# Two loads for x of tile 0, and the first k weights and router weights on ScalarE's queue

## The chip, the core and the metric

The kernel runs on one core of a Trainium2 chip. The metric is the device time of the whole kernel in microseconds (us). TensorE (PE) multiplies, VectorE (DVE), ScalarE (ACT) and GpSimd (POOL) do the elementwise work, and SyncE (SP) mostly issues DMAs; ScalarE can issue DMAs too, on a queue of its own. Both queues feed the same 16 DMA engines of the core.

## The reference

The input x has 2048 rows of 640 values in bf16. It is normalized, goes through linear attention with 32 heads of 20 values, and the rows that a small router picks get an expert's output added. What is computed, in short:

```python
xn = layernorm(x)
q, k, v = split(xn @ wqkv)               # 32 heads of 20
pq, pk = phi(q), phi(k)                  # phi(t) = where(t > 0, t + 1, exp(t)) + 1e-6
num = pq @ (pk^T v);  den = pq . sum(pk)  # for each head
A = (num / (den + 1e-6)) @ wo
r = x @ w_r                              # router: the 8 rows with the largest r
y = (silu(x_sel @ w_gate) * (x_sel @ w_up)) @ w_down * sigmoid(r_sel)
B = x, with y added to those 8 rows
out = x + A + B
```

## The kernel before

The rows are cut into 16 tiles of 128 (one row for each partition). The instructions of all engines are written out by hand in one function, and each engine executes its own in the order in which they are written; an instruction that waits holds up all that follow it on its engine.

The start, which is where the change lies, does this. The function `ld` (L103) issues every load: on SP's queue the tiles 0, 1 and 2 of x, the first half of the k weights (`wkh[0]`, 320 of 640 columns of tile `wk`), tile 3 of x, the second half of the k weights, then the tiles 4 to 15 by three loads of four tiles. On ScalarE's queue goes the load of the router weights `wr`, five rows of 128 values, 1.2 KB, after the load of the activation tables (L106). The weights are laid on the partitions, five rows of 320 values each; one half is 400 KB. One tile of x is 160 KB.

TensorE begins with matmuls on constants that nobody reads (`warm4`, L121): 512 and 256 columns in f32. Then it transposes `wr` into a column (L133), and a second block of 512 columns of `warm4` follows. ScalarE copies that column into the k weights' tile (L135), behind the second half, so that the products of the second half give the router's value r beside the keys (321 columns instead of 320).

For each tile the layer norm takes VectorE's statistics of the two halves of a row (`ln_a` L151, `ln_b` L154), their sum (`ln_g` L157), ScalarE's Ln and Exp for the inverse deviation (`ln_r` L160 and L161) and VectorE's normalization (`ln_xn` L165). Tiles 0 to 3 are then transposed on TensorE (`tr_mm`, L174) and copied to `xnT` by ScalarE or VectorE (`tr_cp`, L181 and L183); later tiles go through a transposing DMA (L186). `K` (L208) multiplies the transposed tile by the two halves of the k weights, ScalarE takes Exp (L224) and Relu (L227), VectorE joins them to `pk` (L243), and `G` (L248, L253) sums the products of the normalized x and `pk` over all tiles in PSUM.

The order around the start, on TensorE, is: warm-up blocks, `wr`, warm-up block, both transposes of tile 0 and the first of tile 1, `K(0)` with the first half of the weights, and so on:

```python
    warm4(512)
    warm4(256)
    pe.transpose(PS[:, 3, :].bitcast(BF16)[:, 0:KC], wr[:], ident[0:KC, 0:KC])
    warm4(512)
    act.copy(wkh[1][:, :, HW], PS[:, 3, :].bitcast(BF16)[:, 0:KC])
```

After the 16 tiles the kernel computes q, the routing and the expert, the merged output weights and the output, tile by tile, with TensorE busy nearly all the time. None of that is written differently.

Of the kernel before, what the change touches and what calls it, by code (L numbers as in the profile page):

```python
# [7 lines left out]
P = 128  # L8
S = 2048
D = 640  # L10
# [28 lines left out]
def kernel(  # L39
# [13 lines left out]
    pe, dve, act, pool, sp = nc.tensor, nc.vector, nc.scalar, nc.gpsimd, nc.sync  # L53

    x_v = A_x[0].rearrange("(t p) d -> p t d", p=P)
    out_v = out[0].rearrange("(t p) d -> p t d", p=P)
    wqkv_v = A_wqkv.rearrange("(kc p) n -> p kc n", p=P)
# [9 lines left out]
    def st(shape, dt, name, tag=None):  # L67
        return sb.tile(shape, dt, name=name, tag=tag or name)

    XX = st([P, T, 2, D], BF16, "XX")  # L70
# [27 lines left out]
    HW = 320  # L98
    wkh = [wk[:, :, 0:HW], wk[:, :, HW + 64 :]]


    def ld(eng, dst, src):
        eng.dma_start(dst, src)  # L103

    ld(sp, XX[:, 0, 1, :], x_v[:, 0, :])
    act.preload_act_table_set("natural_log_exp_and_others")  # L106
    dve.memset(zero[:], 0.0)
    dve.memset(MVf[:], 0.0)
    wr = st([KC, P], BF16, "wr")
    ld(act, wr[:], B_w_r.rearrange("(kc p) -> kc p", p=P))  # L110
    ld(sp, XX[:, 1, 1, :], x_v[:, 1, :])
    ld(sp, XX[:, 2, 1, :], x_v[:, 2, :])
    ld(sp, wkh[0], wqkv_v[:, :, D : D + HW])
    ld(sp, XX[:, 3, 1, :], x_v[:, 3, :])
    ld(sp, wkh[1][:, :, 0:HW], wqkv_v[:, :, D + HW : 2 * D])
    for a, b in ((4, 8), (8, 12), (12, 16)):
        ld(sp, XX[:, a:b, 1, :], x_v[:, a:b, :])
    sp.dma_start_transpose(xnT[:, 0:4, S - P : S], zero[:])

# [820 lines left out]
```

## Time and profile before

| what | value |
|---|---|
| time, median of 3 runs | 106.92 us (106.86 to 107.23) |
| the profiled execution | 107.24 us, of which the span of the trace is 105.5 us |
| TensorE busy | 100.8 us (96%) |
| VectorE, ScalarE, GpSimd busy | 82.5, 69.1, 17.1 us |
| chain that ended last | TensorE 89%, DMA 5% |
| SP's queue, ScalarE's queue | 19.42 MB in 22536 packets, 0.05 MB in 186 packets |

Times in the profile are microseconds from the start of the span; a mean or a duration of one instruction is in ns where it stands without a point. PE is the matmul side of TensorE and PEld its weight loads; a matmul's record is longer than its distance to the next one, since they are pipelined. SPq and ACTq are the DMA issues of SP and ScalarE: their length is that of the issuing instruction, not that of the transfer. In square brackets stands for how long the engine sat idle before the instruction, and what released it. A row with "x3" merges three instructions that follow each other.

### The profile page before, as it was taken

The page shows a single profiled execution, that of the slowest core. Times are in us where ns is not written, and L with a number is a line of the kernel's source. Part 1 is how long each engine was busy: PE and PEld are TensorE (multiplying, and loading weights), DVE is VectorE, ACT ScalarE, POOL GpSimd, SP SyncE. Part 2 cuts the span into 40 slices and gives each one's busy share as a digit, 9 for nine tenths or more (in the row PEclk, how much of TensorE's full clock was granted, in tenths as well). Part 3 has the DMA queues.
Part 4 walks back from the last instruction along what each step waited for, and adds up shares of the span by engine and source line. Part 5 has one row for each costly group of instructions (what it writes and reads, how often), then busy time and mean ns, then how long its engine had stood idle before and what let it go on. Part 6 is the DMA issues. An engine that isn't in the chain of part 4 may idle for free.

```text
span 105.5 us, 2548 instructions
## 1 busy us (share of the span) xinstructions
PE 100.8 (96%) x916; PEld 63.7 (60%) x924; DVE 82.5 (78%) x187; ACT 69.1 (65%) x171; POOL 17.1 (16%) x60
## 2 busy tenths in 40 slices
PE   6989999999999999999999999999999999999980
PEld 3356666666666666667556555655567767777760
DVE  1886999988888898873798995727988997888870
ACT  4359965666666666888597999978993997000000
POOL 7800000430000000000000583300002400000500
PEclk9999999999999999999999999999999999999999
DMA  2899947333555775889998999911630125896343
GB/s 83 228 336 378 319 74 57 77 65 79 117 134 122 115 132 123 185 245 365 237 402 253 362 349 383 321 46 50 229 132 9 29 90 182 193 356 220 124 128 124
DMA packets 23023, 19.65 MB, mean 186 GB/s; under 512 B 10594, under 2 KB 21474, under 8 KB 23010
## 3 DMA queue, kind: packets, MB, share of 16 engines
q1 hardware_dynamic: 22536, 19.42, 64.5%
q8 instruction: 7, 0.11, 0.5%
q0 software_dynamic: 288, 0.01, 0.3%
q10 hardware_dynamic: 186, 0.05, 0.2%
q14 instruction: 6, 0.05, 0.2%
HBM read 13.80 MB, written 3.65 MB: 165 GB/s over the span
## 4 chain that ended last, share of the span: by engine, by line
PE 89%; DMA 5%; issue 1%; SPq 1%; DVE 1%; DVEq 0%
PE PS L208 21%; PE PS L474 21%; PE PS L739 19%; PE PS L248 15%; DMA wk<-in_A_wqkv_dram 5%; PE PS L253 4%; PE PS L695 2%; PE PS L655 1%; SPq L103 1%; PE PS L538 1%; PE PS L717 1%; PE PS L267 1%; PE PS L666 1%; PE PS L174 1%; DVE o L752 1%
## 5 line engine op out<-in xcount | busy, mean ns | idle before, releaser
L208 PE MATMUL PS<-wk,xnT 128*128 128x320 bf16 (+1 forms) x160 | 25.2, 300 | 0.5 <-DMA wk<-in_A_wqkv_dram 0.5
L248 PE MATMUL PS<-pk,XX 128*128 128x512 bf16 x75 | 22.7, 379 | 0.0
L474 PE MATMUL PS<-xnT,wq 128*128 128x512 bf16 x97 | 22.4, 380 | 0.2
L739 PE MATMUL PS<-Mb,pqT 128*128 128x320 bf16 (+4 forms) x165 | 22.1, 295 | 0.0
L224 ACT ACTIVATE ek<-PS 128x320 bf16<-128x320 f32 x32 | 14.1, 441 | 9.9 <-PE PS L208 9.9
L739 PEld LDWEIGHTS <-pqT 128*128 128x128 bf16 x165 | 15.9, 98 | 6.4 <-issue 0.3
L208 PEld LDWEIGHTS <-xnT 128*128 128x128 bf16 x160 | 15.3, 98 | 7.1 <-issue 0.5
L474 PEld LDWEIGHTS <-wq 128*128 128x128 bf16 x100 | 11.4, 118 | 9.1 <-issue 0.2
L243 DVE SCALAR_TENSOR_TENSOR pk<-ek,rk 128x640 bf16<-128x640 bf16 x16 | 13.1, 819 | 4.8 <-ACT rk L227 4.5
L529 DVE SCALAR_TENSOR_TENSOR pqT<-qe,qr 128x512 bf16<-128x512 bf16 x20 | 13.5, 683 | 2.1 <-ACT qr L481 2.0
L480 ACT ACTIVATE qe<-PS 128x512 bf16<-128x512 f32 x20 | 12.2, 609 | 3.3 <-PE PS L474 3.3
L253 PE MATMUL PS<-pk,XX 128*128 128x128 bf16 x64 | 14.0, 219 | 0.3
L227 ACT ACTIVATE rk<-PS 128x320 bf16<-128x320 f32 x32 | 14.0, 437 | 0.0
L248 PEld LDWEIGHTS <-XX 128*128 128x128 bf16 x80 | 7.8, 98 | 8.1
L481 ACT ACTIVATE qr<-PS 128x512 bf16<-128x512 f32 x20 | 12.2, 608 | 0.0
L748 DVE TENSOR_TENSOR o<-PS,XX 128x640 bf16<-128x640 f32 x11 | 9.0, 822 | 2.9 <-PE PS L739 2.0
L198 ACT ACTIVATE XX<-XX,MR,SR 128x640 bf16<-128x640 bf16 x11 | 9.4, 913 | 0.0
L151 DVE BATCH_NORM_STATS2 stats<-XX 128x6 f32<-128x320 bf16 x16 | 7.4, 464 | 2.2 <-DMA XX<-in_A_x_dram 2.2
L165 DVE TENSOR_SCALAR XX<-XX,MVf,SR 128x640 bf16<-128x640 bf16 (+2 forms) x17 | 7.2, 432 | 0.9 <-ACT SR L161 0.9
L259 POOL MEMSET XX<- 128x1 bf16 x18 | 1.9, 108 | 36.0 <-DVE XX L165 14.0
L154 DVE BATCH_NORM_STATS2 stats<-XX 128x6 f32<-128x320 bf16 x16 | 7.7, 479 | 0.0
L253 PEld LDWEIGHTS <-XX 128*128 128x128 bf16 x64 | 6.3, 98 | 0.8
(113 smaller groups left out, 96.0 us busy)
## 6 DMA issues: line engine op xcount, KB each, us to landing
out_dram<-o SPq DMA_DIRECT2D x15, 160.0 KB, 2.0
XX<-in_A_x_dram SPq DMA_DIRECT2D x3, 640.0 KB, 7.8
wg<-in_B_w_gate_dram SPq DMA_DIRECT2D x5, 384.0 KB, 9.1
wu<-in_B_w_up_dram SPq DMA_DIRECT2D x5, 384.0 KB, 6.1
wd<-in_B_w_down_dram SPq DMA_DIRECT2D x1, 1920.0 KB, 10.8
wk<-in_A_wqkv_dram SPq DMA_DIRECT2D x2, 400.0 KB, 5.1
wv<-in_A_wqkv_dram SPq DMA_DIRECT2D x5, 160.0 KB, 3.2
wq<-in_A_wqkv_dram SPq DMA_DIRECT2D x1, 800.0 KB, 5.2
```

The source lines that it names most:

```text
L198: act.activation(XX[:, t, 1, :], XX[:, t, 1, :], AF.Identity, bias=MR[:, t : t + 1], scale=SR1[:, t : t + 1])
L208: pe.matmul(PS[:, b + h, off(t, h) : off(t, h) + w], lhsT=xnT[:, kc, t * P : (t + 1) * P], rhs=wkh[h][:, kc, 0:w], start=(kc == 0), stop=( ...
L224: act.activation(phis[t][0][:, h * HW : (h + 1) * HW], phi_src(t, h, b), AF.Exp)
L227: act.activation(phis[t][1][:, h * HW : (h + 1) * HW], phi_src(t, h, b), AF.Relu)
L243: dve.scalar_tensor_tensor(out=pk[:, t, :], in0=ek[:], scalar=1.0, in1=rk[:], op0=ALU.min, op1=ALU.add)
L248: pe.matmul(PS[:, a, :], lhsT=lhsT, rhs=pk[:, t, 0:512], start=(t == 0), stop=(t == T - 1),)
L253: pe.matmul(PS[:, 5, a * P : (a + 1) * P], lhsT=lhsT, rhs=pk[:, t, 512:D], start=(t == 0 and a == 0), stop=(t == T - 1), skip_group_check= ...
L474: pe.matmul(PS[:, bank, :], lhsT=by5(wq[:, kc, :])[:, m, :], rhs=xnT[:, kc, tb * TBLK : (tb + 1) * TBLK], start=(kc == 0), stop=(kc == KC ...
L480: act.activation(e, PS[:, bank, :], AF.Exp)
L481: act.activation(r, PS[:, bank, :], AF.Relu)
L529: dve.scalar_tensor_tensor(out=pqT[:, m, tb * TBLK : (tb + 1) * TBLK], in0=e, scalar=1.0, in1=r, op0=ALU.min, op1=ALU.add,)
L739: pe.matmul(PS[:, b, o : o + c1 - c0], lhsT=pqT[:, kc, t * P : (t + 1) * P], rhs=Mb[:, kc, c0:c1], start=(kc == 0), stop=(kc == KC - 1))
```

## The change

Tile 0 of x is loaded by two DMAs of 64 partitions, one on SP's queue and one on ScalarE's, there ahead of the load of the activation tables. The first half of the k weights moves from SP's queue to ScalarE's, ahead of the router weights. SP's queue keeps the tiles 1, 2 and 3 of x, now without the k weights between them, and the second half of the k weights. The tiles 8 to 15 come by one load instead of two.

```diff
-    ld(sp, XX[:, 0, 1, :], x_v[:, 0, :])
+    ld(sp, XX[0:64, 0, 1, :], x_v[0:64, 0, :])
+    ld(act, XX[64:P, 0, 1, :], x_v[64:P, 0, :])
     act.preload_act_table_set("natural_log_exp_and_others")
     dve.memset(zero[:], 0.0)
     dve.memset(MVf[:], 0.0)
     wr = st([KC, P], BF16, "wr")
+    ld(act, wkh[0], wqkv_v[:, :, D : D + HW])
     ld(act, wr[:], B_w_r.rearrange("(kc p) -> kc p", p=P))
     ld(sp, XX[:, 1, 1, :], x_v[:, 1, :])
     ld(sp, XX[:, 2, 1, :], x_v[:, 2, :])
-    ld(sp, wkh[0], wqkv_v[:, :, D : D + HW])
     ld(sp, XX[:, 3, 1, :], x_v[:, 3, :])
     ld(sp, wkh[1][:, :, 0:HW], wqkv_v[:, :, D + HW : 2 * D])
-    for a, b in ((4, 8), (8, 12), (12, 16)):
+    for a, b in ((4, 8), (8, 16)):
         ld(sp, XX[:, a:b, 1, :], x_v[:, a:b, :])
     sp.dma_start_transpose(xnT[:, 0:4, S - P : S], zero[:])
```

The diff adds a line to the file, so all lines behind L105 have a number that is one higher after the change.

ScalarE's first instructions in the program before (XX is x, wk the k weights, wr the router weights; in brackets what the instruction waits for):

```order
L106 ACT_TABLE_LOAD
L103 DMA wr<-in_B_w_r_dram 5x128
L135 COPY wk<-PS 128x5 [waits PE_49]
L160 ACTIVATE lnv<-MVf,eps_88 128x1 [waits DVE_49]
L161 ACTIVATE SR<-lnv 128x1 [waits Activation_49]
```

And after the change:

```order
L103 DMA XX<-in_A_x_dram 64x640
L107 ACT_TABLE_LOAD
L103 DMA wk<-in_A_wqkv_dram 128x5x320
L103 DMA wr<-in_B_w_r_dram 5x128
L136 COPY wk<-PS 128x5 [waits PE_49]
L161 ACTIVATE lnv<-MVf,eps_88 128x1 [waits DVE_49]
L162 ACTIVATE SR<-lnv 128x1 [waits Activation_49]
```

The issue of wr has moved from first to third on ScalarE's queue; the copy that needs the transposed wr, and the layer norm behind it, stand in the same order.

SP's first instructions before (DMAHW0_49 and the like are the semaphores of earlier DMAs, of which there are eight in turn):

```order
L103 DMA XX<-in_A_x_dram 128x640 x3
L103 DMA wk<-in_A_wqkv_dram 128x5x320
L103 DMA XX<-in_A_x_dram 128x640
L103 DMA wk<-in_A_wqkv_dram 128x5x320
L103 DMA XX<-in_A_x_dram 128x4x640
L103 DMA XX<-in_A_x_dram 128x4x640 [waits DMAHW0_49]
L103 DMA XX<-in_A_x_dram 128x4x640 [waits DMAHW1_49]
```

And after:

```order
L103 DMA XX<-in_A_x_dram 64x640
L103 DMA XX<-in_A_x_dram 128x640 x3
L103 DMA wk<-in_A_wqkv_dram 128x5x320
L103 DMA XX<-in_A_x_dram 128x4x640 [waits DMAHW0_49]
L103 DMA XX<-in_A_x_dram 128x8x640 [waits DMAHW1_49]
```

One load of k weights has gone from between the loads of x, and the load of tiles 4 to 7, the ninth DMA of the program instead of the eighth, now waits until the first half of tile 0 has landed.

TensorE's, VectorE's and GpSimd's instructions stand in the same order before and after. On TensorE the transpose of wr waits for wr's DMA, as before:

```order
L121 MATMUL PS<-const-float32-0.0 128x512
L121 MATMUL PS<-const-float32-0.0 128x256
L133 LDWEIGHTS wr [waits DMAHW3_49]
L133 MATMUL PS<-ident,wr 128x5 [waits Pool_49]
L121 MATMUL PS<-const-float32-0.0 128x512
L174 LDWEIGHTS XX [waits DVE_49]
```

This is the program before; in the program after, the same rows have line numbers higher by one, and the third waits for DMAHW7_49, the semaphore that wr's DMA has there.

## The prediction

> **What bounds the kernel now.** I read the page first, then the chain that ended last in order of time, then the timelines of the first 8 us engine by engine, then the DMA issues.
>
> The page's head, and the first steps of the chain (start, length, what):
>
> ```profile
> span 105.5 us, 2548 instructions
> PE 100.8 (96%) x916; PEld 63.7 (60%) x924; DVE 82.5 (78%) x187; ACT 69.1 (65%) x171; POOL 17.1 (16%) x60
> ...
> 0.81 0.40 SPq L103
> 1.21 0.06 issue
> 1.27 0.42 SPq L103
> 1.73 0.42 SPq L103
> 2.20 4.88 DMA wk<-in_A_wqkv_dram
> 7.12 0.43 PE PS L208 x2
> ```
>
> TensorE is the bound. Before 7.12 us the chain is not TensorE's: it is SP issuing three x loads one after the other and then the load of the first half of the k weights, which takes 4.88 us to land. Afterwards TensorE hardly rests. In the table by stretches (busy time of each engine) it is busy 12.77 of the 12.88 us that follow:
>
> ```profile
> 7.12:20.00 12.88, 12.77 (x98) 8.30 (x100) 11.32 (x29) 10.26 (x36) 0.76 (x8) 1.00 0.79 196
> 20.00:52.00 32.00, 31.79 (x232) 20.41 (x235) 24.94 (x62) 22.14 (x67) 2.88 (x17) 1.00 0.67 155
> ```
>
> So whatever moves the first product of K(0), now at 7.12, moves the end by nearly the same amount, and nothing later has the slack to give it back. The question is only when that product starts. TensorE's and its weight loader's timelines up to it:
>
> ```profile
> 3.67 0.18 PE L133 MATMUL PS<-ident,wr 5*128 5x5 bf16 x1
> 3.79 2.08 PE L121 MATMUL PS<-const-float32-0.0 128*128 128x512 f32 x2
> 5.65 0.95 PE L174 MATMUL PS<-ident,XX 128*128 128x128 bf16 x7
> 7.12 0.43 PE L208 MATMUL PS<-wk,xnT 128*128 128x320 bf16 x2 [0.52 <-DMA wk<-in_A_wqkv_dram]
> ...
> 5.41 0.93 PEld L174 LDWEIGHTS <-XX 128*128 128x128 bf16 x7 [1.12 <-DVE XX L165]
> 6.54 0.10 PEld L208 LDWEIGHTS <-xnT 128*128 128x128 bf16 x1 [0.20 <-ACT xnT L181]
> ```
>
> TensorE works in written order: the small transpose of the router weights wr (L133), the second warm-up block (L121), the transposes of x (L174), then K. The transposed x is there at 6.54; the k weights keep TensorE idle for 0.52 us, and that is all that an earlier wk can win. ScalarE's part:
>
> ```profile
> 0.80 1.28 ACT L106 ACT_TABLE_LOAD   x1 [0.80 <-PEq L924]
> 0.83 0.58 ACTq L103 DMA_DIRECT2D wr<-in_B_w_r_dram  x1
> 3.89 0.18 ACT L135 COPY wk<-PS 128x5 bf16<-128x5 bf16 x1 [1.81 <-PE PS L133]
> ```
>
> wr is issued at 0.83 and never keeps TensorE waiting: L133 at 3.67 follows the first warm-up block. The copy L135 waits for L133, and the layer norm's Ln and Exp of tile 0 stand behind it on ScalarE.
>
> **The change part by part.** First what the loads cost now, from the timeline of SP's issues and from the DMA issues of short windows (count, KB each, us from issue to landing; issued at 1.27, 2.20, 2.68 and 3.24):
>
> ```profile
> 2.20 0.43 SPq L103 DMA_DIRECT2D wk<-in_A_wqkv_dram  x1
> 2.68 0.52 SPq L103 DMA_DIRECT2D XX<-in_A_x_dram  x1
> 3.24 0.43 SPq L103 DMA_DIRECT2D wk<-in_A_wqkv_dram  x1
> ...
> XX<-in_A_x_dram SPq DMA_DIRECT2D x1, 160.0 KB, 2.3
> wk<-in_A_wqkv_dram SPq DMA_DIRECT2D x1, 400.0 KB, 4.9
> XX<-in_A_x_dram SPq DMA_DIRECT2D x1, 160.0 KB, 4.8
> wk<-in_A_wqkv_dram SPq DMA_DIRECT2D x1, 400.0 KB, 5.4
> ...
> 2.20:5.01 2.81, 2.81 (x6) 0.94 (x4) 1.96 (x7) 0.68 (x3) 2.52 (x9) 1.00 0.91 234
> 5.00:7.12 2.12, 1.61 (x9) 0.89 (x8) 2.06 (x7) 1.50 (x5) 0.30 (x2) 1.00 1.09 335
> ```
>
> The second row of the middle part and the third differ in one thing: the 160 KB of tile 1 stand behind a load of their own size and land 2.3 us after their issue; the 160 KB of tile 3 stand behind wk on the same queue and take 4.8 us, landing at 7.48, 0.4 us after wk (2.20 + 4.9 = 7.1). A small load behind a large one on one queue lands with or after the large one. The change puts wr in exactly that place: its 1.2 KB go out on ScalarE's queue behind half of x's tile 0 and behind wk's 400 KB.
>
> *x of tile 0 in two halves.* Two loads of 64 partitions instead of one of 128. VectorE's first statistics wait for it:
>
> ```profile
> 3.02 0.49 DVE L151 BATCH_NORM_STATS2 stats<-XX 128x6 f32<-128x320 bf16 x1 [1.76 <-DMA XX<-in_A_x_dram]
> ```
>
> A gain here is hidden: the second warm-up block holds TensorE up to 5.65, and L174's weights were there at 5.41. If the halves land later, up to 0.2 us is hidden now, and more if wr is late. I cost it at nothing.
>
> *wk on ScalarE's queue.* Issues there take 0.58 us by the wr row, 0.43 by the wk row; so the half of x goes out at 0.83, wk at about 1.3 to 1.5 instead of 2.20, and wr at 1.8 to 2.1 instead of 0.83. The table load doesn't hold them up: wr's issue ran beside it. Then wk shares the DMA engines with tiles 0 to 3 of x on SP's queue. Bounds for its landing: 2.3 us after the issue like a lone x load (3.7), or 5.4 like the second half of wk (6.9). In between, by volume: 640 KB of x and 400 KB of wk are 1.06 MB; packets of SP's queue flow from about 1.8 (the row below is the window from 1.7 to 2.1 us: packets, MB, share of 16 engines), and at 234 to 335 GB/s this takes 3.2 to 4.5 us, so 5.0 to 6.3. I take 5.8, nearest to the upper rows, since the second half of wk joins before the end.
>
> ```profile
> q1 hardware_dynamic: 36, 0.05, 56.3%
> ```
>
> *wr behind it.* It lands when wk does, at L = 5.8 instead of in time for 3.67. Now everything on TensorE is in order behind L133: L133 at L + 0.05, the warm-up block 0.12 later, L174 at L133 + 1.98 (5.65 − 3.67), K at L174 + 0.95 (from 5.65 to 6.60, where the seven transposes end and xnT is there). Together K starts at L + 2.98 = 8.78, with wk long landed. Against 7.12 that is **+1.66 us**. ScalarE's copy, Ln, Exp and VectorE's normalization, queued behind L133 too, need L135's 0.18, then 5.41 − 3.89 = 1.52 us from copy to L174's weights, and are ready before the warm-up block is through: they add nothing.
>
> *The clock.* The warm-up block exists to keep TensorE busy. The same transposes of 128x128 have two durations, up to 6.3 us (first group) and from 7.4 (second), each row giving count, duration in ns and the starts of the first and last:
>
> ```profile
> L174 PE MATMUL PS<-ident,XX x7: 314/314/314, 5.7 to 6.3; 128*128 128x128 bf16 x7
> L174 PE MATMUL PS<-ident,XX x3: 218/219/219, 7.4 to 7.5; 128*128 128x128 bf16 x3
> L121 PE MATMUL PS<-const-float32-0.0 x6: 634/1061/1222, 0.8 to 4.8; 128*128 128x512 f32 x4, 128*128 128x256 f32 x2
> ```
>
> The granted-clock column reads 1.00 in both stretches, so these durations are the evidence: the full rate came between 6.3 and 7.4, 2.5 to 3.6 us after the second warm-up block's start at 3.79. After the change TensorE idles from 3.7 to 5.85 and the block starts at 5.97; the full rate then comes at 8.5 to 9.6, and K, from 8.78, runs up to 0.8 us at about half rate, which costs 0 to 0.4 us. I take **+0.2**, the middle.
>
> *The rest.* SP loses one issue ahead of tiles 1 to 3, so these and the second half of wk go out about 0.5 us earlier; with K at 8.78 this buys nothing (the second half of wk landed at 3.24 + 5.4 = 8.64 even before). The load of tiles 4 to 7 now waits for the first half of x, which lands about when SP gets there. Tiles 8 to 15 come as one load of 1280 KB; the ninth L151 is tile 8's:
>
> ```profile
> L151 DVE BATCH_NORM_STATS2 stats<-XX x9: 440/486/496, 3.0 to 19.1; 128x6 f32<-128x320 bf16 x9
> ...
> 3.72 2.86 SPq L103 DMA_DIRECT2D XX<-in_A_x_dram  x3
> XX<-in_A_x_dram SPq DMA_DIRECT2D x1, 640.0 KB, 8.9
> ```
>
> It ran at 19.1. The last of the three 640 KB loads, issued before 6.6, landed 8.9 us later, by 15.5 at the latest; the same bytes in two loads land about then, and over 3 us of cover hide them. Nothing.
>
> **The sum.** 1.66 + 0.2 = +1.9 us. The profiled execution took 107.24 us (span 105.5 and 1.7 around it), so it would give 109.1; it lies 0.3 above the median of 106.92, and I put the forecast on the median: **108.8 us**. With L between 5.0 and 6.9 it is 107.8 to 109.9.
>
> **The rivals.**
>
> *wr slips past wk (faster).* Should its few packets not be held by the 400 KB, L133 stays at 3.67 and only the 0.52 us in front of K goes: 106.92 − 0.5 = 106.4. It decides at L = 4.14: below that K starts no later than 7.12. For it: wr has five rows only, and no trace shows a small load behind a large one on ScalarE's queue. Against: the 4.8 us of tile 3 on SP's queue.
>
> *Nothing arrives sooner or later (same).* The bytes before K are the same, and the transfer share was 0.91 and 1.09 of 16 engines from 2.2 to 7.1 us: a second queue adds no engine. wk then lands near 7.1 still, and wr, if its packets get in between the others, before 3.7: 106.9. The Trainium skill says as much (DMA: Bandwidth & Descriptors, Rules for kernel authors): two transfers of disjoint partition halves serialize on the same engines and are not worth it, and spreading loads over issuing engines saves only issue time. The 0.91 agrees; the issue rows (three of about 0.45 us ahead of wk) show why the saved issue time may still count here.
>
> *The clock falls back (slower still).* If the idle 2.2 us wipe out what TensorE had earned, the count starts anew at 5.97. Before, the full rate came 5.5 to 6.6 us after the first warm-up matmul at 0.8 (the last row of that fence); so it would come at about 12, and K's products from 8.78 would run 3.2 us at half rate, losing 1.6: 106.92 + 1.66 + 1.6 = 110.2. For it: TensorE was busy almost all the time from 0.8 and still needed until after 6.3. Against: the gap is less than half of that. The Trainium skill (TensorE: Matmul & The Clock Gate, Part 1) has a free-running window of about 3.4 us that must be busy before the clock is released; by that the release would come at the end of the first busy window after 5.97, an estimate of 9.4 to 12.8, costing 0.3 to 2.0 us; the trace shows no window's edges.
>
> **How the numbers follow.** About 0.5% is what a measurement of this kernel can tell from no change, so faster is below 106.4, slower above 107.45. The forecast has 0.76, of which 0.04 (L just above 4.1) counts as same; wr slipping past 0.10 (0.08 faster, 0.02 same); nothing moves 0.07 (same); the clock falls back 0.07 (slower). Faster 0.08, same 0.02 + 0.07 + 0.04 = 0.13, slower 0.72 + 0.07 = 0.79. The range from 106.9 to 110.0 leaves out the gain and the worst of the clock, together under 0.2.
>
> **What would show it.** In the profile after: the transpose of wr at 5 to 7 us instead of 3.67, its weight load put down to the DMA of wr; the x transposes 2 us behind it; the copy of wr on ScalarE waiting until then; K's first product at 8 to 10 us with no wait on wk, which landed around 6; and all later stretches as they were. It is wrong if the transpose of wr stays near 3.7, or if TensorE after K(0) makes up more than a few tenths.

## The result and the profile after

| what | before | after |
|---|---|---|
| time, median | 106.89 us (106.57 to 107.23) | 111.52 us (109.73 to 112.55), 4 runs |
| ratio to before | | 1.034 (95% interval 1.027 to 1.040) |
| the profiled execution | 107.24 us, span 105.5 | 112.55 us, span 110.8 |
| first product of K | 7.12 us | 11.39 us |

Slower, by 4.6 us in the medians and by 3.6 us by the ratio, where 1.9 was forecast; the median is outside the range. The times after scatter far more than those before, and the ratio leaves out the highest of them as slow runs, so both are given. The profile after is that of the highest of the four times.

TensorE's timeline in that profile, start, length and what it waited for:

```profile
8.52 0.18 PE L134 MATMUL PS<-ident,wr 5*128 5x5 bf16 x1 [4.78 <-DMA wr<-in_B_w_r_dram]
8.63 2.08 PE L122 MATMUL PS<-const-float32-0.0 128*128 128x512 f32 x2
10.50 0.95 PE L175 MATMUL PS<-ident,XX 128*128 128x128 bf16 x7
11.39 0.71 PE L209 MATMUL PS<-wk,xnT 128*128 128x320 bf16 x2
11.89 0.53 PE L175 MATMUL PS<-ident,XX 128*128 128x128 bf16 x3
12.21 2.63 PE L209 MATMUL PS<-wk,xnT 128*128 128x320 bf16 x12
```

TensorE idles 4.78 us for wr, whose transpose now runs at 8.52 instead of 3.67. Behind it come the warm-up block and the transposes of x at the old distance, and K follows without the old wait for wk. The last row is the second loss: the same twelve products of K take 2.63 us, where the profile before has

```profile
7.56 1.86 PE L208 MATMUL PS<-wk,xnT 128*128 128x320 bf16 x12
```

ScalarE's issues, its copy of wr and VectorE's first work after:

```profile
0.81 0.60 ACTq L103 DMA_DIRECT2D XX<-in_A_x_dram  x1
1.48 0.82 ACTq L103 DMA_DIRECT2D wk<-in_A_wqkv_dram  x1
2.34 0.68 ACTq L103 DMA_DIRECT2D wr<-in_B_w_r_dram  x1
8.74 0.18 ACT L136 COPY wk<-PS 128x5 bf16<-128x5 bf16 x1 [6.00 <-PE PS L134]
3.56 0.49 DVE L152 BATCH_NORM_STATS2 stats<-XX 128x6 f32<-128x320 bf16 x1 [2.30 <-DMA XX<-in_A_x_dram]
9.37 0.99 DVE L166 TENSOR_SCALAR XX<-XX,MVf,SR 128x256 bf16<-128x256 bf16 x3 [3.82 <-ACT SR L162]
```

The chain that ended last shows the change in two rows; wr's load takes the place that wk's had:

```profile
2.34 6.14 DMA wr<-in_B_w_r_dram
8.70 2.01 PE PS L122 x2
```

In the table by stretches (busy times of PE, PEld, DVE, ACT and POOL, then granted clock, DMA share, GB/s) the clock falls:

```profile
3.70:7.08 3.38, 0.04 (x1) 0.00 (x0) 1.81 (x6) 0.00 (x0) 1.30 (x4) 1.00 0.96 285
7.08:13.90 6.82, 5.38 (x22) 2.98 (x23) 3.24 (x10) 3.43 (x13) 0.20 (x2) 0.50 1.15 329
13.90:20.00 6.10, 6.10 (x52) 4.27 (x51) 4.90 (x14) 5.20 (x19) 0.20 (x2) 1.00 0.01 3
```

After 3.4 us in which TensorE did next to nothing it is granted half its clock, for 6.8 us, and K's first products at 11.39 fall into that time.

### The profile page after: what moved, and what is told of

It is laid out like the page before. It is cut to its first block, busy times and chain, and to the rows that moved or that the text cites. A ratio compares the mean times of both kernels' runs of the same rounds, so it can differ in the third digit from the quotient of the medians.

```text
span 110.8 us, 2558 instructions
## 1 busy us (share of the span) xinstructions
PE 102.3 (92%) x924; PEld 64.5 (58%) x924; DVE 82.5 (74%) x187; ACT 69.1 (62%) x171; POOL 17.3 (16%) x60
## 4 chain that ended last, share of the span: by engine, by line
PE 88%; DMA 6%; issue 1%; ACT 1%; DVE 1%; ACTq 1%; DVEq 0%
PE PS L209 21%; PE PS L475 20%; PE PS L740 18%; PE PS L249 16%; DMA wr<-in_B_w_r_dram 6%; PE PS L254 3%; PE PS L122 2%; PE PS L696 2%; PE PS L175 1%; PE PS L656 1%; PE PS L539 1%; PE PS L718 1%; PE PS L268 1%; ACT L107 1%; PE PS L667 1%
## 5 line engine op out<-in xcount | busy, mean ns | idle before, releaser
L209 PE MATMUL PS<-wk,xnT 128*128 128x320 bf16 (+1 forms) x160 | 26.2, 308 | 0.0
L249 PE MATMUL PS<-pk,XX 128*128 128x512 bf16 x80 | 23.5, 379 | 0.0
```

What stands on the lines that cost most here:

```text
L209: pe.matmul(PS[:, b + h, off(t, h) : off(t, h) + w], lhsT=xnT[:, kc, t * P : (t + 1) * P], rhs=wkh[h][:, kc, 0:w], start=(kc == 0), stop=( ...
L249: pe.matmul(PS[:, a, :], lhsT=lhsT, rhs=pk[:, t, 0:512], start=(t == 0), stop=(t == T - 1),)
```

## The experiments

**wr first.** The two loads on ScalarE's queue exchanged:

```diff
-    ld(act, wkh[0], wqkv_v[:, :, D : D + HW])
     ld(act, wr[:], B_w_r.rearrange("(kc p) -> kc p", p=P))
+    ld(act, wkh[0], wqkv_v[:, :, D : D + HW])
```

> The changed kernel with the two loads on ScalarE's queue exchanged: wr goes out ahead of the k weights, everything else as changed. Theory 1 (the whole loss is that wr stands behind the k weights and TensorE, in order, waits for it): the transpose of wr is back at 3.7 us, TensorE waits only for the k weights, whose landing was 7.1 before and 8.3 after, so K starts at 6.6 to 8.3 and the time is 106.4 to 108.2, most likely 107. Theory 2 (the k weights or x arrive too late on two queues): the loss stays for the most part, 109 to 111.5.

Measured: 110.16 us median, 107.74 to 112.02; ratio 1.029 (1.022 to 1.037). A miss for theory 1 in its strong form. Its profiled run, of 107.74 us:

```profile
3.68 0.18 PE L134 MATMUL PS<-ident,wr 5*128 5x5 bf16 x1
6.29 0.99 PE L175 MATMUL PS<-ident,XX 128*128 128x128 bf16 x7 [0.72 <-DVE XX L166]
7.64 0.43 PE L209 MATMUL PS<-wk,xnT 128*128 128x320 bf16 x2 [0.37 <-DMA wk<-in_A_wqkv_dram]
wk<-in_A_wqkv_dram ACTq DMA_DIRECT2D x1, 400.0 KB, 5.3
```

wr no longer holds TensorE, but the transposes of x are 0.64 us late and wk lands at 7.6: it is now the third issue on ScalarE's queue, at 2.30. So wr's place isn't the only loss. This profile is of the lowest of the four times; the others, 109.61, 110.70 and 112.02, have no trace (their mean granted clocks were 0.984, 0.984 and 0.969), and what they lost is not shown.

**wr behind wk, alone.** The kernel before, with wr's load on SP's queue right behind the first half of wk:

```diff
-    ld(act, wr[:], B_w_r.rearrange("(kc p) -> kc p", p=P))
     ld(sp, wkh[0], wqkv_v[:, :, D : D + HW])
+    ld(sp, wr[:], B_w_r.rearrange("(kc p) -> kc p", p=P))
```

> The kernel before, with one thing moved: the load of wr goes on SP's queue right behind the first half of the k weights, nothing on ScalarE's. Theory 1: this alone brings most of the loss; wr lands at or after 7.1 us with the k weights, the transpose of wr follows, K starts 3 us behind it at 10 or later: 109.5 to 111.5. Theory 2 (the split of x or the sharing of two queues): wr's place costs little, 107 to 107.5.

Measured: 109.83 us, 109.41 to 110.29; ratio 1.025 (1.020 to 1.030). With nothing split and nothing on a second queue, wr's place alone costs most of the loss. wr was expected at 7.1 or later with wk; it was there at 6.1, and wk landed at 6.2 here (4.0 us from its issue):

```profile
6.12 0.18 PE L133 MATMUL PS<-ident,wr 5*128 5x5 bf16 x1 [2.38 <-DMA wr<-in_B_w_r_dram]
8.98 0.72 PE L208 MATMUL PS<-wk,xnT 128*128 128x320 bf16 x2
9.81 2.71 PE L208 MATMUL PS<-wk,xnT 128*128 128x320 bf16 x12
```

Against the profiled run before, K starts 1.86 us later and the time, 110.29, is 3.05 us longer: the other 1.19 us come behind K's start, with all twelve products at the slow rate.

**wr's transpose later on TensorE.** All loads as changed; the transpose stands ahead of `K(1, (0,), 4, KA)`, the copy ahead of `ln_r(2)`, both through another bank of PSUM:

```diff
-    pe.transpose(PS[:, 3, :].bitcast(BF16)[:, 0:KC], wr[:], ident[0:KC, 0:KC])
-    act.copy(wkh[1][:, :, HW], PS[:, 3, :].bitcast(BF16)[:, 0:KC])
...
+    pe.transpose(PS[:, 5, :].bitcast(BF16)[:, 0:KC], wr[:], ident[0:KC, 0:KC])
     K(1, (0,), 4, KA)
+    act.copy(wkh[1][:, :, HW], PS[:, 5, :].bitcast(BF16)[:, 0:KC])
     ln_r(2)
```

> The changed kernel with all its loads; only the transpose of wr and the copy of its result are written later: on TensorE ahead of K(1) with the first half of the weights, on ScalarE behind the four copies of the transposed tiles. Theory 1: wr still lands at 5.5 to 8.5 us, but the warm-up block, tile 0's layer norm and its transposes no longer stand behind it; K(0) starts when the k weights land, 6.7 to 8.3, and the time is 106.6 to 108.5. If instead the late arrival of the k weights and not the order on TensorE is the loss, K(0) starts no earlier than 10 and the time stays at 110 or more.

Measured: 108.37 us, 107.45 to 109.11; ratio 1.015 (1.007 to 1.023). The loads go out as in the changed kernel, and over half of the loss goes, since tile 0's transposes and K no longer stand behind wr. wk landed at 6.5 in this profile, which is of the lowest time; when wr landed isn't seen, as at 8.03 nothing waits for it:

```profile
6.26 0.99 PE L173 MATMUL PS<-ident,XX 128*128 128x128 bf16 x7 [0.81 <-DVE XX L164]
7.09 0.44 PE L207 MATMUL PS<-wk,xnT 128*128 128x320 bf16 x2
8.03 0.17 PE L358 MATMUL PS<-ident,wr 5*128 5x5 bf16 x1
```

So it is the order on TensorE that turns a late wr into a late K. Two of the four times, 109.07 and 109.11, still lie 2 us above before; they have no trace.

**The gap filled.** The changed kernel with five more warm-up blocks ahead of wr's transpose:

```diff
     warm4(256)
+    for _ in range(5):
+        warm4(256)
     pe.transpose(PS[:, 3, :].bitcast(BF16)[:, 0:KC], wr[:], ident[0:KC, 0:KC])
```

> The changed kernel with five more warm-up blocks of 256 columns between the first warm-up blocks and the transpose of wr: TensorE is busy for 2.4 us (full clock) to 4.8 us (half clock) of the time in which it waited for wr. Theory 1 with the clock falling back as its second part: wr lands as late as in the changed kernel and K starts 2 to 3 us after it, but the granted clock stays full or the transposes and K's first products run at the distance of the full clock, so 0.7 to 1.9 us of the loss go: 109.3 to 110.8 against 111.5. If the clock plays no part, the time stays within 0.5 us of the changed kernel.

Measured: 110.16 us, 109.92 to 110.97; ratio 1.031 (1.025 to 1.037), 1.4 us under the changed kernel's median. The transposes of x and the products run at the full rate, and K starts 2.01 us behind wr's transpose instead of 2.87:

```profile
7.38 0.17 PE L136 MATMUL PS<-ident,wr 5*128 5x5 bf16 x1
9.39 0.43 PE L211 MATMUL PS<-wk,xnT 128*128 128x320 bf16 x2
9.83 1.86 PE L211 MATMUL PS<-wk,xnT 128*128 128x320 bf16 x12
PE PS L211 <- DMA xnT<-XX: 0.5, 1, 0.5
```

The last row, from its waits, is new: TensorE waits 0.5 us for the transposing DMA of a later tile, which it never did in the four profiles of the changed kernel. Why it comes here is not shown.

**The split, alone.** The kernel before with x's tile 0 in two halves:

```diff
-    ld(sp, XX[:, 0, 1, :], x_v[:, 0, :])
+    ld(sp, XX[0:64, 0, 1, :], x_v[0:64, 0, :])
+    ld(act, XX[64:P, 0, 1, :], x_v[64:P, 0, :])
```

> The kernel before with the split of x's tile 0 alone: 64 partitions on SP's queue, 64 on ScalarE's ahead of the table load, then wr; the k weights and the rest stay on SP's queue. What the runs have shown so far: with the split the halves landed at 3.45 us instead of 2.99, and in the run with wr first VectorE got the transposes' input to TensorE 0.6 us later. Theory A (the split delays the layer norm by its two issues and the shared engines): tile 0 lands at 3.3 to 3.5, the first transpose is at 6.0 to 6.3 instead of 5.65, TensorE idles between warm-up and transposes, K at 7.1 to 7.6: 106.9 to 107.6 where the clock stays full, 1.7 more where it falls to half for 3.4 us. Theory B (the split costs nothing, the k weights on ScalarE's queue do): 106.9, with the landings of before.

Measured: 107.76 us in ten runs; ratio 1.006 (1.003 to 1.009). Theory A: VectorE's first statistics at 3.54 instead of 3.02, and wr, issued behind the half, holds its transpose to 4.12. The profile is of the highest of the ten times, 108.74; K starts only 0.38 us later than before in it, and its twelve products, at 8.30, take 2.40 us.

```profile
3.54 0.50 DVE L152 BATCH_NORM_STATS2 stats<-XX 128x6 f32<-128x320 bf16 x1 [2.28 <-DMA XX<-in_A_x_dram]
4.12 0.10 PEld L134 LDWEIGHTS <-wr 5*128 5x128 bf16 x1 [1.10 <-DMA wr<-in_B_w_r_dram]
8.30 2.40 PE L209 MATMUL PS<-wk,xnT 128*128 128x320 bf16 x12
1.47 0.96 ACTq L103 DMA_DIRECT2D wr<-in_B_w_r_dram  x1
```

**wk on ScalarE's queue, alone, behind wr.** The kernel before with one line moved:

```diff
     ld(act, wr[:], B_w_r.rearrange("(kc p) -> kc p", p=P))
+    ld(act, wkh[0], wqkv_v[:, :, D : D + HW])
...
-    ld(sp, wkh[0], wqkv_v[:, :, D : D + HW])
```

> The kernel before with the first half of the k weights alone moved to ScalarE's queue, behind wr; x is not split. Theory A (the split is what remains of the loss when wr goes first): tile 0 lands at 3.0 again, the first transpose is at 5.65, and K starts with the k weights, which share the engines with x: 6.6 to 7.3, so 106.4 to 107.1. Theory B (the k weights on the second queue slow x down): tiles 0 and 1 land later than 3.0 and 3.6, the first transpose is at 6 or later, and the time is 107.3 to 110 as with wr first and the split.

Measured: 106.56 us in ten runs against 107.12; ratio 0.996 (0.994 to 0.998). This version beats both kernels. wk goes out at 1.45, lands at 6.0, and K waits for nothing:

```profile
1.45 0.41 ACTq L103 DMA_DIRECT2D wk<-in_A_wqkv_dram  x1
wk<-in_A_wqkv_dram ACTq DMA_DIRECT2D x1, 400.0 KB, 4.6
3.68 0.18 PE L133 MATMUL PS<-ident,wr 5*128 5x5 bf16 x1
6.54 0.45 PE L208 MATMUL PS<-wk,xnT 128*128 128x320 bf16 x2
```

**wr first, and the gap filled.** "wr first" with one `warm4(256)` more behind the second warm-up block.

> The kernel with wr issued ahead of the k weights and all else as changed, with one more warm-up block of 256 columns behind the second, so that TensorE has work from 5.6 to 6.1 (full clock) or 6.5 (half). Its twin without the block had four times from 107.7 to 112.0. If these come from the clock that falls back because TensorE rests, the block keeps it up: all runs at 107.3 to 108.5, with a mean granted clock of 1.000. If they come from loads that land late in some runs, the spread stays.

Measured: 109.91 us, 109.30 to 111.45; ratio 1.026 (1.021 to 1.032). A miss: the block does not help, and in the profiled run K waits for wk, not for the clock:

```profile
2.47 0.43 ACTq L103 DMA_DIRECT2D wk<-in_A_wqkv_dram  x1
wk<-in_A_wqkv_dram ACTq DMA_DIRECT2D x1, 400.0 KB, 6.4
8.89 0.43 PE L210 MATMUL PS<-wk,xnT 128*128 128x320 bf16 x2 [2.02 <-DMA wk<-in_A_wqkv_dram]
```

With the split, wk or wr has to be third on ScalarE's queue. In these two profiles the third, wk, lands at 7.6 and 8.9, against 6.0 where it is second and x is whole. The 2.02 us that K waits here is a late landing; the granted clock reads 1.00 throughout.

**The good version, filled.** "wk on ScalarE's queue" with `warm4(128)` behind the second warm-up block.

> The kernel before with the k weights on ScalarE's queue behind wr, x not split, and 128 more columns in a warm-up block of its own behind the second. If the clock is at risk there too, this one has 106.4 to 107.2 in all runs while its twin without the block scatters; if the clock is not at risk, the two are alike within 0.4 us, this one up to 0.4 slower, since the block may hold the first transpose.

Measured: 107.64 us in ten runs; ratio 1.005 (1.002 to 1.009), 1.1 us above its twin. A miss: the twin doesn't scatter, and here K starts no later (6.48), but TensorE then waits 0.7 us for the transposing DMA at 17 us, as in "the gap filled". Why these blocks bring that wait about, and what the rest of the 1.1 us is, was not settled.

**Not split, wr still behind wk.** The changed kernel with x's tile 0 whole on SP's queue.

> The changed kernel without the split: tile 0 of x whole on SP's queue, and on ScalarE's queue the k weights first and wr behind them. So far: the split alone cost 0.6%, the k weights alone on ScalarE's queue gained 0.4%, wr behind the k weights alone cost 2.5%, and K starts 2.9 us after wr's landing. If wr's place behind the k weights is the cause and the split only adds to it: the k weights go out at 0.8 instead of 1.5, land with wr at 5 to 6, K starts at 8 to 9, and the time is 108.3 to 110.5, below the changed kernel but far above before. If the split is the cause: 106.4 to 107.3.

Measured: 109.13 us, 108.29 to 109.44; ratio 1.018 (1.012 to 1.025). The split adds to the loss, wr's place makes it: with no half of x ahead, wk and wr go out and land a good us earlier.

```profile
5.20 0.18 PE L133 MATMUL PS<-ident,wr 5*128 5x5 bf16 x1 [1.46 <-POOL bm L285]
8.06 0.72 PE L208 MATMUL PS<-wk,xnT 128*128 128x320 bf16 x2
8.89 2.33 PE L208 MATMUL PS<-wk,xnT 128*128 128x320 bf16 x12
```

The wait is put down to GpSimd, which had long been done; the DMA of wr is the other thing that this matmul waits for.

**wr behind both halves of wk.** The changed kernel with the second half of wk moved to ScalarE's queue too, between the first half and wr.

> The changed kernel with the dose doubled: both halves of the k weights, 800 KB, go on ScalarE's queue ahead of wr. If wr's landing sets the time, it lands after the second half, at 7.5 to 9.5 where the changed kernel's typical run has 6.3 to 6.7 and the profiled one 8.5; K starts 2.9 us later, at 10.4 to 12.4, and the time is 111.5 to 114. If something else in the changed kernel sets it, the time stays within 0.7 us of the changed kernel's 111.5.

Measured: 112.33 us, 111.65 to 113.22; ratio 1.052 (1.044 to 1.061).

```profile
8.54 0.18 PE L134 MATMUL PS<-ident,wr 5*128 5x5 bf16 x1 [4.79 <-DMA wr<-in_B_w_r_dram]
11.40 0.66 PE L209 MATMUL PS<-wk,xnT 128*128 128x320 bf16 x2
12.07 1.86 PE L209 MATMUL PS<-wk,xnT 128*128 128x320 bf16 x12
```

This run took 111.75 us. wr and K stand where they stood in the first profile of the changed kernel, which took 112.55; here the twelve products run at the full rate.

**The changed kernel again**, three times, since its median lay 2 us above what wr's usual landing gives.

> The changed kernel itself once more, for the spread of its times and a second profile. In the first profile wr landed at 8.5, where 6.3 and 6.7 were seen in two variants with the same loads. If the late landing was an accident of that run, this profile has 6 to 7 and K at 9 to 10, and the times are 109.5 to 111.5; if it belongs to the kernel, 8 or more again.

> The changed kernel a third time, one look, as the run before: wr at 6 to 7 if the first profile was an accident, 8 or more if not; in either case K starts 2.9 to 3.0 us after wr has landed if the clock is at half rate, 2.0 if it is full.

> The changed kernel again, for the two groups of its times: of nine so far, four lie at 109.3 to 109.7 and five at 111.3 to 112.6. Either cause, the clock at half rate or a late wr, leaves both groups here.

Measured: 109.29 to 111.71 (four runs), 109.41 (one), 109.55 to 112.62 (six; ratio 1.038, 1.033 to 1.044). The three profiles have wr's transpose at 6.27, 6.31 and 6.18 and K 2.86 or 2.87 us behind. All three are of low times (109.29, 109.41, 109.55), so how late wr lands in the high ones is seen in the first profile alone. The first of the three:

```profile
6.27 0.18 PE L134 MATMUL PS<-ident,wr 5*128 5x5 bf16 x1 [2.53 <-DMA wr<-in_B_w_r_dram]
8.25 0.95 PE L175 MATMUL PS<-ident,XX 128*128 128x128 bf16 x7
9.14 0.54 PE L209 MATMUL PS<-wk,xnT 128*128 128x320 bf16 x2
9.68 1.86 PE L209 MATMUL PS<-wk,xnT 128*128 128x320 bf16 x12
wk<-in_A_wqkv_dram ACTq DMA_DIRECT2D x1, 400.0 KB, 4.6
```

Here the full rate came in time for the twelve products, and the run took 109.29 us. Of the 15 times of the changed kernel six lie at 109.3 to 110.3 and nine at 111.2 to 112.6. Each run's mean granted clock is on record. The three highest times, 112.55, 112.61 and 112.62, have 0.969, which is what half a clock for 6.82 of 110.8 us makes; 109.52, 109.73 and 110.33 have 0.984; the other nine, three of them at 109.3 to 109.6 and six at 111.2 to 111.7, have 1.000. So three high times share the first profile's fall of the clock, and for the other six the column shows none. That does not make theirs a full rate: "wr behind wk, alone" has 1.000 too, with its products at the slow rate.

**The gap filled, beside the changed kernel.**

> The changed kernel with the five warm-up blocks ahead of wr's transpose again, beside the changed kernel itself. If the upper group of the changed kernel is the half-rate clock after TensorE's rest, this one has no time above 111.2, as in its four runs so far (109.9 to 111.0). If the upper group is wr landing 2 us later in some runs, the blocks can't help there, and about half of these times are at 111 to 112.5 too.

Measured: 110.59 us, 109.50 to 110.97; ratio 1.034 (1.029 to 1.038). With the four above that is ten times, none above 111.0, where the changed kernel has nine of 15; and all ten have a granted clock of 0.998 or more, where six of those 15 have 0.984 or less. So the clock no longer falls when TensorE has something to do while it waits. In the profile, of 109.50 us, the weight load still waits for wr, K follows wr's transpose (6.70) by 2.00 us, and the wait for a later tile's transposing DMA is back (0.6 us):

```profile
6.69 0.09 PEld L136 LDWEIGHTS <-wr 5*128 5x128 bf16 x1 [0.52 <-DMA wr<-in_B_w_r_dram]
8.70 0.43 PE L211 MATMUL PS<-wk,xnT 128*128 128x320 bf16 x2
```

What was expected of a late wr does not hold: the blocks would help there too, since K then follows by 2.0 us and not by 2.87. With wr's transpose at 8.52, K would start at 10.5, 1.8 us later than here: an estimate of 110.7 to 111.3 us, the lower one if the 0.6 us of waiting go. The highest of the ten is 110.97. So the filled gap does not tell a clock at half rate from a late wr.

## Why the prediction was right and wrong

*Right: the mechanism and its distance.* wr goes out behind wk, and TensorE, in order, starts K a fixed time after wr. The prediction had 2.93 us from wr's transpose to K (1.98 + 0.95). Measured: 2.87 (8.52 to 11.39), 2.87 (6.27 to 9.14), 2.86 (6.12 to 8.98), 2.86 (5.20 to 8.06), 2.86 (8.54 to 11.40). Like the rows that it was taken from, this is a distance with the transposes at the slow rate; with the gap filled it is 2.0. Where the twelve products run at the full rate the time follows K's start: in the run of 109.29 us K is 2.02 us later than before and the time 2.05 us longer than the 107.24 of the profiled run before; behind both halves of wk 4.28 later and 4.51 longer. That nothing behind gives it back held, too. The low times came out near the sum, 109.1 for a profiled execution against 109.29, 109.41 and 109.55, in part because two small misses went against each other: K came 0.26 to 0.40 us later than 8.78, and the clock cost less than 0.2 us in two of the three.

*Failed: L, the landing of wr.* "It lands when wk does, at L = 5.8", with 6.9 as the upper bound, is the step that misses most in the profile of 112.55 us. wr's transpose came at 8.52 and K at 11.39 instead of 8.78: 2.61 of the 3.45 us by which that run lies above 109.1. wk took 6.8 us from its issue there, and 4.6, 4.6 and 5.5 in the other three profiles of the changed kernel; the bound was taken from one run of one load.

```profile
wk<-in_A_wqkv_dram ACTq DMA_DIRECT2D x1, 400.0 KB, 6.8
```

The issues do not explain it. They were taken as 0.43 to 0.58 us each and took 0.60, 0.82 and 0.68, so that wr went out at 2.34 and not at 2.1; but it went out at 2.34 in the run of 109.55 us too, and its transpose was at 6.18 there. What made wk and wr late in the first profile stays open. Nor is "lands when wk does" exact: in the run of 109.55 us wr was there 0.8 us before wk, which landed at 7.0. The rows that the prediction compares for it (they are the first and the third of the fence's middle part, not the second and the third) differ in more than their place: tile 3 was also issued 1.4 us later than tile 1, with more under way. That wr's place behind wk is what delays it is shown by moving wr alone, not by those rows.

*Mis-sized: the clock term.* The prediction assumed that the full rate comes 2.5 to 3.6 us after the warm-up block starts and cost it at 0.2 us; the clock falling back was a rival with 0.07. In the first profile the rate came 5.3 us after the block (8.63 to 13.90), and K was at half rate for 2.5 us: 0.77 us on the twelve products alone, 1.04 from K's start, which came 4.27 us later, to the time, which grew by 5.31. That is the other 0.84 us of the miss: the rival came true in this run, on top of a late wr. In the three low profiles the same difference was 0.03, 0.11 and 0.39 us. The rule cited from the Trainium skill beside that rival (TensorE: Matmul & The Clock Gate, Part 1: a free-running window of about 3.4 us) agrees with the first profile: the granted clock stays at 0.50 for 6.82 us, twice 3.41.

*What is open: the median.* No profile shows a run of 111.2 to 111.7 us, where six of the 15 times lie; the median of 111.52 is between two of them. K's products at the slow rate cost 0.91 to 1.19 us behind K's start in the three profiles in which wr's late landing went with them (1.04; wr behind wk, alone, 1.19; not split, 0.91). With wr's usual landing, that is an estimate of 110.1 to 110.5 us, too little. A wr at 8.54 with the products at the full rate took 111.75, behind both halves of wk. So the traces point to a wr later than 6.3 in those six runs as well; none of them shows it, and what the clock added there stays open.

*Failed: the split "costs nothing".* Alone it costs 0.6%: in its profile tile 0 is there 0.5 us later, not earlier. In the changed kernel its first part is hidden behind wr, but the half of x pushes wk and wr back by an issue, and that is in L (wr's transpose at 5.20 without the split, 6.2 with it).

*The rivals.* wr slipping past wk, so that its transpose stays at 3.67, did not happen in any profile. "Nothing arrives sooner" was half right: the second queue did bring wk earlier, from 7.1 to 6.0, when it was second there and x was whole; in the changed kernel it landed at 8.3, 6.1, 6.1 and 7.0. The Trainium skill's rule on disjoint partition halves (DMA: Bandwidth & Descriptors, Rules for kernel authors) is borne out by the split's 0.6%, though here it does harm, where the rule has it as merely useless; its rule that a second issuing engine saves only issue time agrees with the 0.4% of wk moved alone.

## What to carry to other kernels

A tiny load that an in-order engine waits for early goes ahead of large loads on its queue; its size says nothing about its landing, what stands before it does. When a wait moves, ask what the idle engine loses beside the time: TensorE's clock is a term of its own: here it added 1.04 us to a K that came 4.27 us later, and 1.19 us to one that came 1.86 us later. When a kernel's times fall into groups, ask which group a profile is from before taking it for the usual run. To move one load to the other queue was worth 0.4% here, to put half of x and wk there ahead of wr cost 3.4%: issues on a queue are serial, and what is third goes out at 2.1 to 2.5 us, where the first goes out at 0.8.

## What was not expected of the hardware

The issue of one and the same load varies: that of wk took 0.82 us on ScalarE's queue in the first profile, 0.57 in the run of 109.29 us and 0.41 when it stood behind wr with x whole. Some single load lands up to 2 us after the usual (wr's transpose at 8.52 against 6.2 with the same loads); why was not found. And the granted-clock column read 1.00 before 6.6 us in the profile before, although the transposes ran at about half rate there (seven of them in 0.95 us, 314 ns each, against 218 ns from 7.4 us on): at the start of a trace the instructions' own durations are the evidence, not the column.
